# Loading x for TensorE's first transposes by 128-column blocks, with the first products between the transposes

## The chip, the cores and the metric

The kernel runs on one core of a Trainium2 chip. The metric is the device time of one execution in microseconds, lower is better. Each execution also leaves a span (first to last instruction, some 1.7 to 1.9 us less than the device time) and the mean TensorE clock that was granted. One execution of each kernel is profiled; all moments below are microseconds from the start of that profile's span.

## The reference, cut to what matters

```python
B, S, D, F = 32, 32, 1024, 3584          # bf16
def reference(x, w_gate, w_up, w_down):
    return (gelu(x @ w_gate) * (x @ w_up)) @ w_down
```

The tokens are 32 x 32 = 1024 rows. The kernel computes the products with one level of a Strassen-like scheme. The change touches the first 6 us alone.

## The kernel before

The products take x with its columns (d) on the partitions. Most of x is transposed while it is loaded. Such a load takes long (the first, issued at 2.2, has landed at 6.8), so the first 256 columns that are needed (KQ = 2 blocks of 128) are loaded as they lie, and TensorE transposes them: 4 row blocks x 2 column blocks = 8 transposes. VectorE and ScalarE copy the results from PSUM, the memory in which the transposes leave them, to `b21`. Six matmuls on constants (NWARM) run while these loads are on their way. The code is abridged; cuts are marked.

```python
NB = 512; P = 128; NB_P = 4; HALF = 2; KQ = 2; KB = 4; NWARM = 6
x_nat = spool.tile([P, NB_P, KQ * P], bf16, name="x_nat", tag="s1")
# SyncE's queue loads token rows 0..255, ScalarE's 256..511; both column blocks at once
for eng, p0, p1 in ((nc.sync, 0, HALF), (nc.scalar, HALF, NB_P)):
    eng.dma_start(out=x_nat[:, p0:p1, :], in_=xf[p0*P : p1*P, KD*P : (KD+KQ)*P].rearrange(...))
# ... (cut)
for k, eng in enumerate((nc.sync, nc.scalar)):
    load_ahead(0, k, k + 1, eng)            # weights a12a of k = 0 and k = 1
for which, eng in enumerate((nc.sync, nc.scalar)):
    load_w(eng, 0, which, KD, KD + KQ)      # first w_gate and w_up tiles
# ... (further loads cut)
for _ in range(NWARM):
    nc.tensor.matmul(warm_ps, lhsT=ones_w, rhs=ones_m, start=True, stop=True)
tags = iter("CCBB")
for dt in range(KQ):
    for half in range(2):
        tp = ps1.tile([P, HALF * P], bf16, name="tp", tag=next(tags), ...)
        for b in range(HALF):
            nc.tensor.transpose(tp[...], x_nat[:, half*HALF + b, dt*P : (dt+1)*P], ident)
        (nc.vector.tensor_copy, nc.scalar.copy)[half](b21[:, dt, ...], tp)
# ... (helpers cut)
ps = [acc(t) for t in "CCAA"]
for k in range(KQ):
    for cols in (first 256 tokens, last 256 tokens) if k == 0 else (all 512,):
        for j in range(KB):
            product_ahead(ps[j], 0, j, k, k + 1, cols)   # one matmul: a12a(k, j) x b21(k)
plain0(KD, KD + KQ)                          # first w_gate products, then w_up
```

The banks matter: `ps[0]` and `ps[1]` take the two C banks that the first two transposed halves used, so product j=1 cannot start before the second half has been copied.

## Time and profile before

| | before |
|---|---|
| time, median of 3 runs | 275.15 us (275.04 to 275.26) |
| span of the profiled run | 273.2 us |
| TensorE (PE) busy | 98% |
| first transpose / first product / first w_gate product | 3.49 / 4.34 / 6.35 us |
| full clock granted (clock record of the trace) | 4.89 us |

These are lines of the profile's page (the span, the busy table, and the summary of the chain of work that ended last).

```profile
span 273.2 us, 3351 instructions
...
PE 268.9 (98%) x1202; PEld 188.4 (69%) x1202; DVE 193.8 (71%) x194; ACT 112.1 (41%) x183; POOL 107.1 (39%) x55
...
PE 98%; ACT 0%; issue 0%
```

TensorE is the limit from end to end. The next fence is the timeline of TensorE in the head of the kernel before: start, duration, engine, line of the kernel, operation, output <- inputs, shape, type, count. Line L232 holds the transposes, L272 the first products, L239 the first w_gate and w_up products.

```profile
start us, us, engine line op out<-in xcount [idle before <-releaser]
2.86 0.63 PE L224 MATMUL psA<-const-bfloat16-1.0 128*128 128x512 bf16 x1
3.49 1.05 PE L232 MATMUL tp<-ident,x_nat 128*128 128x128 bf16 x8
4.34 0.63 PE L272 MATMUL psC<-b,a12a 128*128 128x256 bf16 x2
4.77 0.44 PE L272 MATMUL psA<-b,a12a 128*128 128x256 bf16 x2
5.05 0.38 PE L272 MATMUL psC<-b,a12a 128*128 128x256 bf16 x2
5.26 0.38 PE L272 MATMUL psA<-b,a12a 128*128 128x256 bf16 x2
5.48 0.59 PE L272 MATMUL psC<-b,a12a 128*128 128x512 bf16 x2
...
6.35 0.59 PE L239 MATMUL psA<-b,wg 128*128 128x512 bf16 x2
```

Read the starts, not the durations: matmuls overlap (a transpose is shown with 0.29 to 0.31 us, the next starts 0.107 us after it), and the end of one is modelled. Before the grant, transposes start 0.107 us apart and half-width products (256 tokens) 0.213 us apart. At full clock the distances are 0.055 and 0.109 us, half of that, so the state before the grant is called half clock here. Two products take 0.43 us at 4.34 and 0.22 us at 5.05: full clock was granted in between, at 4.89. The sixth warm-up starts at 2.86 and streams for 0.427 us (the distance between the starts of the warm-ups), to 3.29. So TensorE idled for 0.2 us before the first transpose, waiting for x:

```profile
PEld L232 <- DMA x_nat<-in_x_dram: 0.9, 1, 0.9
```

(From the table of waits: the weight load of the first transpose waited 0.9 us in total for the load of x, once; most of it passed while warm-ups still streamed.)

In the rest of this text, "idle" means TensorE's idle time between the last warm-up and the first w_gate product. It is computed from the starts and from the streaming times above, not from the modelled ends.

### The profile page before, as it was taken

The page shows a single profiled execution, that of the slowest core. Times are in us where ns is not written, and L with a number is a line of the kernel's source. Part 1 is how long each engine was busy: PE and PEld are TensorE (multiplying, and loading weights), DVE is VectorE, ACT ScalarE, POOL GpSimd, SP SyncE. Part 2 cuts the span into 40 slices and gives each one's busy share as a digit, 9 for nine tenths or more (in the row PEclk, how much of TensorE's full clock was granted, in tenths as well). Part 3 has the DMA queues.
Part 4 walks back from the last instruction along what each step waited for, and adds up shares of the span by engine and source line. Part 5 has one row for each costly group of instructions (what it writes and reads, how often), then busy time and mean ns, then how long its engine had stood idle before and what let it go on. Part 6 is the DMA issues. An engine that isn't in the chain of part 4 may idle for free.

```text
span 273.2 us, 3351 instructions
## 1 busy us (share of the span) xinstructions
PE 268.9 (98%) x1202; PEld 188.4 (69%) x1202; DVE 193.8 (71%) x194; ACT 112.1 (41%) x183; POOL 107.1 (39%) x55
## 2 busy tenths in 40 slices
PE   8999999999999999999999999999999999999994
PEld 4444777877877677676868686754447888888883
DVE  0268997986655676766658556459999999999511
ACT  2262665454643646555463636430300023962001
POOL 1000099999796794949577575000000000000000
PEclk9999999999999999999999999999999999999999
DMA  7994321423505505050514280005992445696202
GB/s 189 239 258 133 105 71 44 118 62 94 156 14 140 146 8 157 0 154 3 153 36 119 57 291 1 0 2 163 353 292 79 132 137 187 217 284 196 78 0 78
DMA packets 53249, 33.77 MB, mean 124 GB/s; under 512 B 8688, under 2 KB 53232, under 8 KB 53232
## 3 DMA queue, kind: packets, MB, share of 16 engines
q1 hardware_dynamic: 50240, 31.07, 39.7%
q10 hardware_dynamic: 2992, 2.49, 2.8%
q8 instruction: 9, 0.15, 0.2%
q14 instruction: 8, 0.07, 0.1%
HBM read 29.62 MB, written 2.10 MB: 116 GB/s over the span
## 4 chain that ended last, share of the span: by engine, by line
PE 98%; ACT 0%; issue 0%
PE psA L257 34%; PE psA L431 18%; PE psC L257 17%; PE psC L431 7%; PE psB L431 7%; PE psB L257 5%; PE psB L239 3%; PE psA L239 3%; PE psC L272 2%; PE psA L272 1%; PE psA L224 1%; PE tp L232 0%; ACT o_sb L571 0%
## 5 line engine op out<-in xcount | busy, mean ns | idle before, releaser
L257 PE MATMUL psA<-t,s 128*128 128x512 f32 x208 | 54.2, 402 | 0.0
L249 ACT ACTIVATE h<-c 128x512 bf16<-128x512 f32 x52 | 31.7, 627 | 37.4 <-DVE c L335 37.4
L257 PEld LDWEIGHTS psA<-t,s 128*128 128x128 f32 x208 | 39.1, 188 | 9.3
L162 POOL TENSOR_TENSOR s<-wu 128x1024 fp32r<-128x1024 bf16 x12 | 26.1, 2179 | 25.0 <-PE psC L257 16.8
L335 DVE TENSOR_TENSOR c<-sn,psA 128x512 f32<-128x512 f32 x26 | 17.7, 682 | 16.5 <-PE psA L257 14.6
L257 PEld LDWEIGHTS <-wg 128*128 128x128 bf16 x168 | 15.4, 98 | 20.2 <-issue 3.4
L163 POOL TENSOR_TENSOR s<-s,wg 128x1024 fp32r<-128x1024 f32 x12 | 27.4, 2284 | 0.9
L165 POOL TENSOR_TENSOR s<-wg,wu 128x1024 fp32r<-128x1024 bf16 x12 | 27.1, 2255 | 0.0
L340 ACT COPY sn<-psA 128x512 f32<-128x512 f32 x42 | 23.7, 584 | 7.9 <-PE psA L257 7.8
L257 PE MATMUL psA<-t,a22r 128*128 128x512 f32 x104 | 25.9, 391 | 0.0
L257 PE MATMUL psC<-t,s 128*128 128x512 f32 x104 | 25.8, 390 | 0.0
L257 PE MATMUL psC<-b22r,s 128*128 128x512 f32 x104 | 25.7, 389 | 0.0
L340 ACT COPY sn<-psC 128x512 f32<-128x512 f32 x26 | 15.2, 588 | 24.5 <-PE psC L257 22.7
L257 PE MATMUL psA<-b,wg 128*128 128x512 bf16 x104 | 24.6, 380 | 0.0
L257 PEld LDWEIGHTS psC<-t,s 128*128 128x128 f32 x104 | 19.4, 188 | 4.4 <-ACT ahead L362 0.3
L257 PEld LDWEIGHTS psA<-t,a22r 128*128 128x128 f32 x104 | 19.5, 188 | 4.1
L257 PEld LDWEIGHTS psC<-b22r,s 128*128 128x128 f32 x104 | 19.5, 188 | 4.1
L335 DVE TENSOR_TENSOR c<-sn,psC 128x512 f32<-128x512 f32 x26 | 17.7, 687 | 6.2 <-PE psC L257 6.2
L354 DVE TENSOR_TENSOR hi<-h,psA 128x512 bf16<-128x512 bf16 x14 | 9.6, 687 | 13.2 <-PE psA L257 13.2
L164 POOL TENSOR_TENSOR s<-wg,s 128x1024 fp32r<-128x1024 bf16 x8 | 17.2, 2155 | 0.6
L410 DVE TENSOR_TENSOR lo<-c,h 128x512 bf16<-128x512 f32 x12 | 16.9, 1405 | 0.6
L410 DVE TENSOR_TENSOR hi<-c,h 128x512 bf16<-128x512 f32 x14 | 16.9, 1205 | 0.5
(95 smaller groups left out, 398.5 us busy)
## 6 DMA issues: line engine op xcount, KB each, us to landing
wu<-in_w_up_dram SPq DMA_DIRECT2D x13, 512.0 KB, 4.1
wdb<-in_w_down_dram SPq DMA_DIRECT2D x12, 512.0 KB, 4.7
wdb<-in_w_down_dram SPq DMA_DIRECT2D x12, 384.0 KB, 4.2
wg<-in_w_gate_dram SPq DMA_DIRECT2D x8, 512.0 KB, 5.2
v<-in_w_down_dram SPq DMA_DIRECT2D x4, 512.0 KB, 6.1
out_dram<-o_sb ACTq DMA_DIRECT2D x16, 128.0 KB, 1.7
wg<-in_w_gate_dram SPq DMA_DIRECT2D x6, 256.0 KB, 4.5
v<-in_w_down_dram SPq DMA_DIRECT2D x4, 384.0 KB, 7.4
```

Of the source, the lines that this page charges most:

```text
L162: yield eng.tensor_tensor(s1, a21, a22, ADD)
L163: yield eng.tensor_tensor(s2, s1, a11, SUB)
L164: yield eng.tensor_tensor(s4, a12, s2, SUB)
L165: yield eng.tensor_tensor(s3, a11, a21, SUB)
L239: nc.tensor.matmul(ps, lhsT=w_tiles[0, which][:, dt, fl * P : (fl + 1) * P], rhs=x_rows(dt, nb), start=(dt == first), stop=(dt == last),)
L249: nc.scalar.activation(h, src, ACT.Gelu_apprx_tanh)
L257: nc.tensor.matmul(ps, lhsT=lhs[:, k, :], rhs=rhs[:, k, :], start=(start and k == 0), stop=(k == KD - 1), skip_group_check=True,)
L335: tt(t, s, ps, ADD)
L340: nc.scalar.copy(t, ps)
L354: tt(g_of(ft)[:, :NB], h0, psa, MUL)
L410: tt(g_of(ft)[:, NB:], added(sn5[fl], psa[fl]), h1[fl], MUL)
L431: nc.tensor.matmul(banks[m], lhsT=lhs(k)[:, m * P : (m + 1) * P], rhs=rhs(k), start=(start and k == 0), stop=(k == HF - 1), skip_group_che ...
```

## The change

The intent is to begin earlier. Only the first 128-column block of x is needed for the first products, so it is loaded alone, with half the bytes. TensorE transposes it, starts the k = 0 products on the first half of the tokens, transposes the second block, and goes on with the other half. All copies go to VectorE.

```diff
-        for eng, p0, p1 in ((nc.sync, 0, HALF), (nc.scalar, HALF, NB_P)):
+        def load_nat(eng, dt, p0, p1):
             eng.dma_start(
-                out=x_nat[:, p0:p1, :],
-                in_=xf[p0 * P : p1 * P, KD * P : (KD + KQ) * P].rearrange("(b p) d -> p b d", p=P),
+                out=x_nat[:, p0:p1, dt * P : (dt + 1) * P],
+                in_=xf[p0 * P : p1 * P, (KD + dt) * P : (KD + dt + 1) * P].rearrange("(b p) d -> p b d", p=P),
             )
+        load_nat(nc.sync, 0, 0, HALF)
+        load_nat(nc.scalar, 0, HALF, NB_P)
 ...
-        for k, eng in enumerate((nc.sync, nc.scalar)):
-            load_ahead(0, k, k + 1, eng)
+        load_ahead(0, 0, 1)
+        load_nat(nc.scalar, 1, 0, NB_P)
+        load_ahead(0, 1, 2, nc.scalar)
 ...
-        for dt in range(KQ):
+        def transposed(dt):
 ...
-                (nc.vector.tensor_copy, nc.scalar.copy)[half](b21[:, dt, half * hw : (half + 1) * hw], tp)
+                nc.vector.tensor_copy(b21[:, dt, half * hw : (half + 1) * hw], tp)
+        transposed(0)
 ...
         for k in range(KQ):
-            for cols in (slice(0, NB // 2), slice(NB // 2, NB)) if k == 0 else (slice(None),):
+            for half in range(2):
                 for j in range(KB):
-                    product_ahead(ps[j], 0, j, k, k + 1, cols)
+                    product_ahead(ps[j], 0, j, k, k + 1, slice(half * HALF * P, (half + 1) * HALF * P))
+                if k == half == 0:
+                    transposed(1)
```

More of the change, by code (lines that the diff above doesn't have):

```diff
@@ L183 @@
     with tc.manual_schedule():
-        for eng, p0, p1 in ((nc.sync, 0, HALF), (nc.scalar, HALF, NB_P)):
+        def load_nat(eng, dt, p0, p1):
             eng.dma_start(
-                out=x_nat[:, p0:p1, :],
-                in_=xf[p0 * P : p1 * P, KD * P : (KD + KQ) * P].rearrange("(b p) d -> p b d", p=P),
-            )
+                out=x_nat[:, p0:p1, dt * P : (dt + 1) * P],
+                in_=xf[p0 * P : p1 * P, (KD + dt) * P : (KD + dt + 1) * P].rearrange("(b p) d -> p b d", p=P),
+            )
+        assert KQ == 2
+        load_nat(nc.sync, 0, 0, HALF)
+        load_nat(nc.scalar, 0, HALF, NB_P)
         alloc_w(0, 0)
@@ L224 @@
             nc.tensor.matmul(warm_ps, lhsT=ones_w, rhs=ones_m, start=True, stop=True)
-        tags = iter("CCBB")
-        for dt in range(KQ):
+        def transposed(dt):
             for half in range(2):
                 hw = HALF * P
-                tag = next(tags)
+                tag = "CB"[dt]
                 tp = ps1.tile([P, hw], bf16, name="tp", tag=tag, bufs=BANKS[tag])
@@ L282, with plain0 @@
         ps = [acc(t) for t in "CCAA"]
-        tok0 = [(acc("A"), acc("B")) for _ in range(FC)]
-        def plain0(d0, d1):
+        def plain0(tok0, d0, d1):
             for which in (0, 1):
@@ L291 @@
         for k in range(KQ):
-            for cols in (slice(0, NB // 2), slice(NB // 2, NB)) if k == 0 else (slice(None),):
+            for half in range(2):
                 for j in range(KB):
-                    product_ahead(ps[j], 0, j, k, k + 1, cols)
-        plain0(KD, KD + KQ)
+                    product_ahead(ps[j], 0, j, k, k + 1, slice(half * HALF * P, (half + 1) * HALF * P))
+                if k == half == 0:
+                    transposed(1)
+        tok0 = [(acc("A"), acc("B")) for _ in range(FC)]
+        plain0(tok0, KD, KD + KQ)
         for j, copy in enumerate((nc.scalar.copy, nc.vector.tensor_copy) * 2):
@@ L300 @@
             copy(ahead[0][:, j, :], ps[j])
-        plain0(KD + KQ, DT)
+        plain0(tok0, KD + KQ, DT)
         a12_ahead.append(xpool.tile([P, KD, (NAHEAD - 2 * KB) * P], bf16, name="a12b"))
```

## The prediction

> **What bounds the kernel.** TensorE: 98% of the 273.2 us span (engine table), and the chain that ended last is 98% TensorE. From 3.49 us on, its first 25 us hold no wait. So only TensorE's idle or slow-clocked time in the head can change, and what changes there passes through one for one.
>
> **The head before (timeline, tiles, clock record).** Six warm-up matmuls start at 0.77, 0.427 us apart (half clock), and stop streaming at about 3.29. The halves of x land 2.7 and 2.9 us after issue (3.44, 3.63); the first transpose starts at 3.49. Eight transposes, 0.107 us apart, run to 4.34. The first copy (VectorE, 3.92 to 4.21, 0.29 us) hides under later transposes, so the first product starts at 4.34 with no gap. Full clock is granted at 4.89: half-width products go from 0.21 to 0.109 us. The first w_gate product starts at 6.35: my marker.
>
> **What the change does.**
> 1. First x loads: half the bytes, the same number of rows. Packets of 512 B take about 27 ns, of 256 B about 17 ns in this trace, but the first appear only 1.3 us after issue and come slower than the engines could take them, so I expect 0.05 to 0.15 us sooner, not half. [...] The unchanged warm-up ends at 3.29: at most 0.2 us to gain. Transposes start at about 3.40.
> 2. Four transposes stand before the first product, to 3.83. But nothing hides the copy now: second transpose + 0.31 us latency + 0.29 us copy + about 0.06 puts the first product at about 4.2, and its weights, landed at 4.24 before, come no sooner. A new TensorE gap of about 0.4 us. The second bank's copy, on VectorE after the first, ends at about 4.4, roughly as j=1 needs it.
> 3. The other four transposes move behind four half-width products, to about 5.0, at full clock (0.22 instead of 0.43 us). Block 1 of x lands at about 4.6, in time. Its copies hide under four products (0.44 us).
> 4. k=1 products are split: 4 more matmuls, a few ns each.
> 5. k=1 weights and first w_up tile go one place later in the ScalarE queue: about 5.1 (was 4.45) and 6.2 (was 5.78), needed at about 5.7 and 7.4. Later loads had about 0.5 us to spare.
>
> **Sum.** Before full clock TensorE streams for 1.4 us (3.49 to 4.89); after, about 1.08 (3.40 to 4.89 less 0.4). The lost 0.3 us of half-clock work costs 0.16 at full clock, plus small stalls: marker at 6.53 to 6.6. All on the critical path. Time 275.15 + 0.22 = 275.37 us, range 275.05 to 275.9.
>
> **Chances.** Faster by over 2%: 0.005; within 2%: 0.985; slower by over 2%: 0.01.
>
> **What would show it.** Timeline: first transpose 3.35 to 3.45 (1); TensorE idle 0.3 to 0.5 us after the fourth transpose, released by VectorE's copy or the weights (2); no wait at the later transposes (3), none for k=1 weights or w_up (5); marker 0.15 to 0.3 later; then both timelines parallel.
>
> **What would make it wrong.** The clock. [...] here it opened 4.1 us after the first matmul. [...] If it opens earlier or the gap is shorter, the change is level or gains 0.1. Block 1 landing after 5.0 would add its lateness one for one.

The sum came to 275.15 + 0.22 = 275.37 us. Passages are cut from the text, and the cuts marked, where no trace of this case shows what they said: a sentence on packet sizes in step 1, beside the packet times from the trace, and, under what would make it wrong, how the grant comes about and what a delay of it would cost, which was not part of the sum. The expectations of e1, e8 and e11 have cuts of the same kind.

## The result, and the profile after

| | before | after |
|---|---|---|
| time, median of 6 runs each, same rounds | 275.20 us (275.04 to 275.77) | 275.18 us (274.77 to 275.89) |
| ratio, 95% interval | | 0.9999 (0.9983 to 1.0014) |
| first transpose / first product / first w_gate product | 3.49 / 4.34 / 6.35 | 3.29 / 4.09 / 6.16 us |
| full clock granted | 4.89 us | 4.13 us |
| idle | 0.21 us | 0.45 us |

A ratio is the mean time of one kernel's runs over that of the other's of the same rounds, so it is not quite the ratio of the medians.

The page of the changed kernel:

```profile
span 273.0 us, 3360 instructions
...
PE 268.6 (98%) x1206; PEld 188.7 (69%) x1206; DVE 195.3 (72%) x196; ACT 110.9 (41%) x181; POOL 108.1 (40%) x55
...
PE 98%; ACT 0%; DVE 0%; issue 0%
```

TensorE's timeline in its head (here L237 are the transposes, L279 the first products, L246 the w_gate products):

```profile
3.29 0.63 PE L237 MATMUL tp<-ident,x_nat 128*128 128x128 bf16 x4
4.09 0.48 PE L279 MATMUL psC<-b,a12a 128*128 128x256 bf16 x2 [0.17 <-DVE b L240]
4.41 0.38 PE L279 MATMUL psA<-b,a12a 128*128 128x256 bf16 x2
4.62 0.39 PE L237 MATMUL tp<-ident,x_nat 128*128 128x128 bf16 x4
4.85 0.38 PE L279 MATMUL psC<-b,a12a 128*128 128x256 bf16 x2
...
6.16 0.81 PE L246 MATMUL psA<-b,wg 128*128 128x512 bf16 x3
```

The chain of work that ended last, in the same stretch (start, duration, what):

```profile
3.49 0.23 PE tp L237 x2
3.72 0.02 issue
3.74 0.30 DVE b L240
4.04 0.04 issue
4.09 0.48 PE psC L279 x2
```

The reader is to see three things. First, the transposes start as soon as the warm-up lets them, at 3.29. Second, VectorE's copy now stands in TensorE's chain, where before no copy did. The four transposes have streamed by 3.71, and the first product starts at 4.09: 0.37 us idle, and another 0.08 us before product j=1, whose bank waits for the second copy. Third, from the first products on the distances are those of full clock (4.41 to 4.62 for two).

So one number of the comparison is suspect. The changed kernel's w_gate products start 0.19 us earlier although TensorE idled 0.25 us longer, and the clock was granted 0.76 us earlier. The profiled run of the change, 274.77 us, is also the fastest of its six.

### An arithmetic for the head

From the first transpose to the first w_gate product TensorE streams 8 transposes and 16 half-widths: 8 x 0.107 + 16 x 0.213 = 4.27 us at half clock. At full clock each piece takes 0.51 of that (0.109/0.213). With O the moment of the grant, 3.29 the end of the warm-up, and I1 and I2 the idle time before and after O, the first w_gate product (the marker M) starts at

M = O + 0.51 x (4.27 - (O - 3.29 - I1)) + I2.

Before, with O = 4.885: 4.885 + 0.51 x (4.27 - 1.39) = 6.35 (measured 6.35). After, with O = 4.128: 4.128 + 0.51 x (4.27 - 0.47) + 0.08 = 6.15 (measured 6.16). Both fit. With before's O, the change would have reached the marker at 4.885 + 0.51 x (4.27 - 1.14) = 6.48, which is 0.13 later. With the change's O, before would have been at 5.98, which is 0.17 earlier than the change. These two are estimates from the measured numbers.

### The profile page after: what moved, and what is told of

Read it like the earlier page. It is cut to its first block, busy times and chain, and to the rows that moved or that the text cites. A ratio compares the mean times of both kernels' runs of the same rounds, so it can differ in the third digit from the quotient of the medians.

```text
span 273.0 us, 3360 instructions
## 1 busy us (share of the span) xinstructions
PE 268.6 (98%) x1206; PEld 188.7 (69%) x1206; DVE 195.3 (72%) x196; ACT 110.9 (41%) x181; POOL 108.1 (40%) x55
## 4 chain that ended last, share of the span: by engine, by line
PE 98%; ACT 0%; DVE 0%; issue 0%
PE psA L264 34%; PE psA L440 18%; PE psC L264 17%; PE psC L440 7%; PE psB L440 7%; PE psB L264 5%; PE psB L246 3%; PE psA L246 3%; PE psC L279 2%; PE psA L279 1%; PE psA L229 1%; ACT o_sb L580 0%; PE tp L237 0%; DVE b L240 0%
## 5 line engine op out<-in xcount | busy, mean ns | idle before, releaser
L162 POOL TENSOR_TENSOR s<-wu 128x1024 fp32r<-128x1024 bf16 x12 | 27.5, 2294 | 24.4 <-PE psC L264 16.0
L419 DVE TENSOR_TENSOR lo<-c,h 128x512 bf16<-128x512 f32 x12 | 17.9, 1490 | 0.6
L483 ACT COPY snb<-psC 128x512 f32<-128x512 f32 x4 | 2.2, 590 | 36.5 <-PE psC L440 36.5
```

The lines of the kernel that those rows point to most:

```text
L162: yield eng.tensor_tensor(s1, a21, a22, ADD)
L419: tt(g_of(ft)[:, NB:], added(sn5[fl], psa[fl]), h1[fl], MUL)
```

## The experiments

My theory has two parts. The change has the transposes start up to 0.2 us earlier and then idles longer than that, a small net loss. What the two profiles show the other way round is the moment of the clock grant, which is a matter of chance from run to run. The rivals are that the change itself makes the clock open earlier, that the change really gains 0.19 us, or that one of its two parts (loads, order) is a gain by itself. Runs e1 to e4 share their runs of before, and so do e5 to e8, and e9 to e11.

### e1: before again, unedited

> The kernel before, unedited, profiled a second time. My theory: the moment O at which full TensorE clock is granted is a matter of chance [...], and the first w_gate product (the marker M) follows it: M = 0.49 O + 3.97 us, from a first transpose at 3.49 and 4.27 us of half-clock work; O = 4.89 gave 6.35. So O will be another number than 4.89 and M will follow the formula within 0.1 us; the span follows as 273.19 + 0.49 (O - 4.89). Rival: the clock is granted earlier because of the change, then O is 4.89 here again.

Measured: full clock at 6.71 (it was 4.89), the first transpose at 3.28, M = 7.15, idle 0.02 us, span 274.0 us. From TensorE's timeline:

```profile
3.28 1.08 PE L232 MATMUL tp<-ident,x_nat 128*128 128x128 bf16 x8
...
6.71 0.60 PE L272 MATMUL psA<-b,a12a 128*128 128x512 bf16 x2
7.15 0.59 PE L239 MATMUL psA<-b,wg 128*128 128x512 bf16 x2
```

The time of the four runs was 275.13 to 275.85. The same program therefore moves its marker by 0.80 us by itself, and the span with it. My formula gave 7.26; it missed by 0.11 because x had landed at 3.23 instead of 3.44, so nothing was left to wait for. With the idle time as measured, the arithmetic above gives 7.15. What follows: O is not a property of the kernel, and before also can start its transposes the moment the warm-up ends. The head start of the change is 0 to 0.2 us.

### e2: the change again, unedited

> The changed kernel, unedited, profiled a second time. My theory: M = 0.49 O + 4.04 us (first transpose 3.29, a gap of 0.37 us after four transposes), plus up to 0.08 where the second product waits for the second copy; O will not be 4.13 again. At the same O this is 0.07 to 0.16 us later than before. Rival (the change lets the clock open sooner): O is 4.1 again and the marker 6.16. Second rival (the change gains 0.19 us, as the two profiles say): M at the same O lies 0.19 below before's.

Measured: O = 3.92, first transpose 3.28, first product 4.45, M = 6.48, idle 0.80 us, ratio 1.0007 (0.9986 to 1.0028). The size of the gap was wrong here. It was 0.74 us, and in the chain it is the weights, not the copy, that release the first product:

```profile
1.24 3.17 DMA a12a<-in_w_gate_dram
4.41 0.05 issue
4.45 0.39 PE psC L279 x2
```

The load was the same, and was issued at the same moment, as in the first profile of the change, where it landed at 3.73. By the arithmetic, this O and this idle time give 6.47. What follows: the grant came earlier than in the first profile, yet the marker is later. The change is exposed to a second thing: it has only four transposes, not eight, to fill the wait for the first weights. (Before had little to spare either. Its first weights landed at 4.25 and 4.09 in its two profiles, and its first product started at 4.34 and 4.15; by an estimate from these numbers, weights at 4.41 would have made it wait too, with 0.43 us, four transposes, less of idle time.) The rival "O is 4.1 again" is not refuted by this profile, since 3.92 is close to 4.13. It is taken up below the table of all heads.

### e3: the order of the change, the loads of before

```diff
-        load_nat(nc.sync, 0, 0, HALF); load_nat(nc.scalar, 0, HALF, NB_P)
+        for eng, p0, p1 in ((nc.sync, 0, HALF), (nc.scalar, HALF, NB_P)):
+            eng.dma_start(out=x_nat[:, p0:p1, :], ...)     # as before
```

The weights' loads follow in the order of before, too.

> The loads of before (both 128-column blocks of x in one load per half), TensorE's order and the copies of the change. My theory: first transpose at 3.49 as before, then the uncovered copy: a gap of about 0.37 us before the first product, M = 0.49 O + 4.15, 0.18 us later than before at the same O. Rival: the order is the useful part (fewer half-clock transposes), then M is at or below before's 0.49 O + 3.97.

Measured: O = 3.67, first transpose 3.29 (x had landed at 3.12), first product 4.09, idle 0.48 us (0.40 and 0.09, both released by VectorE's copies), M = 6.14; ratio 0.9994 (0.9977 to 1.0011).

```profile
3.29 0.58 PE L232 MATMUL tp<-ident,x_nat 128*128 128x128 bf16 x4
4.09 0.47 PE L274 MATMUL psC<-b,a12a 128*128 128x256 bf16 x2 [0.23 <-DVE b L235]
...
6.14 1.03 PE L241 MATMUL psA<-b,wg 128*128 128x512 bf16 x4
```

The gap came with the order alone, as expected. The first transpose was earlier than expected, because the loads of before landed earlier than in its first profile. My formula for M (5.95) assumed the idle time to lie before the grant, where it costs half; here all of it lay after, where it costs in full. The arithmetic gives 6.13.

### e4: the loads of the change, the order of before

> The loads of the change, TensorE's order and the copies of before. My theory: first transpose at 3.29 as in the change, but the fifth to eighth wait for block 1 (landed at 4.37 in the change): a gap of 0.6 to 0.7 us released by the load of x, M = 0.49 O + 4.2, 0.24 us later than before at the same O. Rival (the split loads alone are a gain of 0.2 us): M at 0.49 O + 3.87.

The edit: the split loads of the diff above, with the eight transposes in a row and the copies of before. Measured: the profiled run took 277.45 us, the four others 275.17 to 275.59; ratio 1.0003 (0.9984 to 1.0022). TensorE's timeline:

```profile
3.28 0.63 PE L237 MATMUL tp<-ident,x_nat 128*128 128x128 bf16 x4
4.91 0.61 PE L237 MATMUL tp<-ident,x_nat 128*128 128x128 bf16 x4 [0.99 <-DMA x_nat<-in_x_dram]
...
8.72 1.06 PE L244 MATMUL psA<-b,wg 128*128 128x512 bf16 x4
```

Block 1 landed at 4.86, so the gap was 1.20 us, not 0.65. The larger loss of the profiled run was elsewhere: full clock came at 8.78, after the whole head, which ran at half clock to its end. In the eight other profiles with six warm-ups the grant came between 3.67 and 6.71. What follows: no gain of the split loads alone was seen. The profile with the most idle time of these nine (1.17 us to the marker) also had the latest grant. That the one led to the other is my estimate; it was not shown (see e8).

### e5 and e6: both kernels with 20 warm-up matmuls

```diff
-    NWARM = 6
+    NWARM = 20
```

> Before with 20 warm-up matmuls instead of 6, so that every load has landed and full clock is granted before the first transpose: what is left is the order alone, at full clock. My theory: from the first transpose to the first w_gate product 2.46 us, of which 0.28 us TensorE idles (the first copy no longer hides under the transposes, which now take 0.45 us). Rival (the order of the change is as good, its gap came from late data): the same distance in the changed kernel. The whole time is longer by the warm-up and of no interest.

> The change with 20 warm-up matmuls. My theory: from the first transpose to the first w_gate product 2.70 us, 0.24 more than before with 20, all of it idle TensorE waiting for VectorE's first two copies (0.5 us in all). Rival: 2.46 us, as before with 20.

This takes away the landings and the grant: all has landed, and full clock is granted before the first transpose in both (3.48 and 6.70). What is left is the order. The lines of TensorE, before with 20:

```profile
6.45 0.61 PE L232 MATMUL tp<-ident,x_nat 128*128 128x128 bf16 x8
7.11 0.46 PE L272 MATMUL psC<-b,a12a 128*128 128x256 bf16 x2
...
8.92 1.03 PE L239 MATMUL psA<-b,wg 128*128 128x512 bf16 x4
```

and the change with 20:

```profile
8.02 0.38 PE L237 MATMUL tp<-ident,x_nat 128*128 128x128 bf16 x4
8.67 0.47 PE L279 MATMUL psC<-b,a12a 128*128 128x256 bf16 x2 [0.27 <-DVE b L240]
...
10.73 0.59 PE L246 MATMUL psA<-b,wg 128*128 128x512 bf16 x2
```

From the first transpose to the marker it is 8.918 - 6.449 = 2.47 us before and 10.728 - 8.019 = 2.71 us in the change (unrounded starts of the trace). Idle is 0.29 and 0.52 us. Expected were 2.46 and 2.70. With the landings and the grant taken out, the new order costs 0.24 us, all of it the uncovered copies. (The device times, 277.64 and 279.37, differ by the grant, which came 3.2 us later in e6 and left its warm-ups slow; single runs, state unknown.)

### e7: the change with 5 warm-up matmuls

> The change with 5 warm-up matmuls: block 0 of x landed at 2.9 in three profiles, the sixth warm-up streams to 3.29. My theory: the first transpose at 2.95 to 3.0, but the first product then waits for its weights (landed at 3.7 to 4.4) as well as for the copy, so it starts no sooner than 3.8: idle 0.5 to 0.9 us before the marker; of the 0.33 us taken out 0.1 at most shows in M, and the time stays within 0.5 us of before. Rival (the warm-up is all that hides the gain): M earlier by 0.17 us at the same O, no more idle time than the 0.45 of the change.

Measured: the profiled run took 277.28 us, the other three 274.97 to 275.27; ratio 1.0014 (0.9975 to 1.0053). The first transpose started at 2.86, 0.43 us earlier (2.95 to 3.0 was expected), and the first product at 4.29:

```profile
2.86 0.63 PE L237 MATMUL tp<-ident,x_nat 128*128 128x128 bf16 x4
4.29 0.61 PE L279 MATMUL psC<-b,a12a 128*128 128x256 bf16 x2 [0.80 <-DMA a12a<-in_w_gate_dram]
...
8.10 1.55 PE L246 MATMUL psA<-b,wg 128*128 128x512 bf16 x4
```

The weights landed at 4.24, so the earlier transposes only made the gap longer: idle 0.97 us, a little above the 0.5 to 0.9 expected, and 277.28 is outside the 0.5 us of before that I expected. Here too full clock came late, at 9.15. What follows: the warm-up does not hide a gain. Before 3.7 to 4.4 there is nothing for TensorE to multiply, since the first weights are not there.

### e8: the change with 2 warm-up matmuls

> The change with 2 warm-up matmuls: they stream to about 1.63, then TensorE idles to 2.95. [...] O lies between 6 and 10, mostly above 7, M between 7.5 and 8.7, and the time is 1 to 1.5 us above before's. Rival (the clock needs no activity beyond a fixed delay after the first matmul): O between 3.4 and 7 as before, and the time within 0.5 us of before's.

Measured: 275.67 to 278.02 us, median 277.08, ratio 1.0077 (1.0048 to 1.0106). The interval lies wholly above 1. O = 6.36 and M = 6.98 in the profiled run, which was the fastest of the four; expected were O between 6 and 10 (right) and M above 7.5 (wrong for this run). The median loss of 1.9 us is larger than the 1 to 1.5 us expected. The rival, a fixed delay after the first matmul with times within 0.5 us of before's, is out. This is the one experiment whose timing alone decides something: warm-up work, which computes nothing, is worth over a microsecond. Why it is so was not shown. The three slower runs were not profiled, and in the profiled run the grant, at 6.36, came within the range seen with six warm-ups, although TensorE idled from about 1.63 (an estimate: two warm-ups of 0.427 us from 0.77) to 2.99. The ground that this expectation gave for its O, M and time is cut; they stand as what was expected, no more.

Does idle time delay the grant? In the eight profiles with six warm-ups and a grant at 3.67 to 6.71, TensorE idled 0.02 to 0.80 us between the last warm-up and the marker. In e4 it idled 1.17 us, and the grant came at 8.78; in e7, with five warm-ups, it was 0.97 us and 9.15. That fits, but idle time alone does not put the grants in order: e1 idled 0.02 us and had 6.71, while the change in its first profile idled 0.37 us before a grant at 4.13. In e5 and e6 TensorE worked through the same warm-ups without a gap, and the grant came at 3.48 and 6.70. What decides the moment of the grant was not shown.

### e9: both blocks of x first, then the weights

```diff
         load_nat(nc.sync, 0, 0, HALF)
         load_nat(nc.scalar, 0, HALF, NB_P)
+        load_nat(nc.sync, 1, 0, HALF)
+        load_nat(nc.scalar, 1, HALF, NB_P)
 ...
-        load_nat(nc.scalar, 1, 0, NB_P)
 ...
         transposed(0)
+        transposed(1)
 ...
-                if k == half == 0:
-                    transposed(1)
```

> Both blocks of x before any weights (each block half on SyncE's and half on ScalarE's queue), eight transposes in a row as before, all copies on VectorE. My theory: block 1 lands by about 3.6, the copies hide again, and the gap that is left is the first weights', now third in their queue (landing 4.2 to 4.8): idle 0.1 to 0.5 us before the first w_gate product, no better than before's 0.02 to 0.21; time the same as before's within its spread of 1 us. Rival (the early block is worth its 0.2 us once the copies are hidden): first transpose 3.29, idle under 0.05, M = 0.49 O + 3.87.

Measured: eight transposes in a row from 3.29, first product at 4.70, idle 0.53 us (0.1 to 0.5 expected), O = 5.30, M = 6.73; ratio 1.0011 (0.9993 to 1.0029).

```profile
3.29 1.06 PE L238 MATMUL tp<-ident,x_nat 128*128 128x128 bf16 x8
4.70 0.61 PE L281 MATMUL psC<-b,a12a 128*128 128x256 bf16 x2 [0.35 <-DVE b L241]
```

Block 1 landed by 3.72 and the transposes ran without a gap, but the first weights, third in SyncE's queue, landed at 4.65. (The line names VectorE, whose fourth copy ended at 4.68. But the first product reads the first copy alone, which had ended at 4.04. And it started 0.046 us after the weights landed, as in e2 and e7, where the weights were the release; after a copy it is 0.052 to 0.053 us, as in the first profile of the change. So it was the weights.) This was my attempt at a version that beats both, and it does not: what is gained on x is given back on the weights.

### e10: the change, with the second half's copies on ScalarE

```diff
-                nc.vector.tensor_copy(b21[:, dt, ...], tp)
+                (nc.vector.tensor_copy, nc.scalar.copy)[half](b21[:, dt, ...], tp)
```

> The change, but the second half's copies on ScalarE as before. My theory: the second copy then ends at about 4.4 instead of 4.25 (ScalarE takes 0.37 us for one, VectorE 0.29), which holds the second product: idle before the marker 0.5 to 0.6 us instead of the change's 0.45 if the weights land by 4.1. Rival (VectorE doing both in turn is what makes the gap): idle below 0.4.

Measured: idle 0.57 us, in the range expected; the second product waited 0.23 us for ScalarE. The size was right, but not for the reason I gave. ScalarE's timeline:

```profile
2.82 1.28 ACT L240 ACT_TABLE_LOAD   x1 [2.82 <-issue]
4.11 0.37 ACT L240 COPY b<-tp 128x256 bf16<-128x256 bf16 x1
```

ScalarE first issues its loads, one more than before, then loads its function table for 1.28 us, and only then can copy, at 4.11. In before's profile the table load ran from 2.26 to 3.54, ahead of the first copy. So moving the copies to VectorE is the part of the change that keeps the fourth load on ScalarE's queue from showing. (One run of 276.05 us, state unknown.)

### e11: the change a third time

> The changed kernel, unedited, profiled a third time and timed in five more rounds. My theory: idle TensorE before the marker 0.45 us when the first weights land by 4.03 and more by their lateness after that (0.80 at 4.41); M follows from idle time and O by the same arithmetic as in all runs, and from M to the last matmul 262.97 to 263.03 us. Of some six runs none or one falls above 276.5 [...]. Rival (the idle time matters only through its own length): no run above 276.0 in any number of runs.

Measured: 274.93 to 275.97 us in six runs, ratio 1.0001 (0.9986 to 1.0016). O = 3.90, M = 6.27, idle 0.58 us, where 0.45 was expected with weights that landed by 4.03 (they had at 3.71): the 0.37 and 0.10 us of the two copies, and 0.09 us before k = 1, whose weights landed at 5.33 (5.10 in the first profile). No run passed 276.0, so a time like the 277.45 of e4 or the 277.28 of e7 was not seen in 16 runs of the change itself, and this experiment does not tell whether idle time matters only through its own length.

### All heads in one table

| profile | O | idle | M measured | M by the arithmetic |
|---|---|---|---|---|
| before | 4.89 | 0.21 | 6.35 | 6.35 |
| before again (e1) | 6.71 | 0.02 | 7.15 | 7.15 |
| after | 4.13 | 0.45 | 6.16 | 6.15 |
| after again (e2) | 3.92 | 0.80 | 6.48 | 6.47 |
| after, third (e11) | 3.90 | 0.58 | 6.27 | 6.25 |
| order only (e3) | 3.67 | 0.48 | 6.14 | 6.13 |
| loads only (e4) | 8.78 | 1.17 | 8.72 | 8.73 |

From M to the last matmul it is 262.97 to 263.04 us in all seven, and in e5, e6, e8 and e10. (The two exceptions are e9 with 263.16 and e7 with 263.50, where the clock came 1 us after M.) Nothing that happens in the head is caught up or made worse later, so idle time and O explain the span.

The three profiles of the change all had an early grant (4.13, 3.92 and 3.90), and the two of before a later one. Taken alone, this fits the rival that the change makes the clock open earlier. The timed runs speak against it. A run's mean granted clock was 0.997 or 0.998 in the profiles whose grant came at 6.36 to 6.71 (e1, e6, e8, e10; the time before a grant counts as 1.00 in this number, as 0 to 4.89 of before's profile does, so what is missing lies at the end: the grant then ended before the span did), and 1.000 in the six profiles with six warm-ups whose grant came at 3.67 to 5.30. Four of the 16 runs of the change show 0.998 (275.89 to 275.97 us, its slowest), and 11 of the 29 runs of before whose clock is listed show 0.997 or 0.998. So the change gets late grants too. Whether it gets them less often cannot be told from so few runs.

## Why the prediction was right or wrong, point by point

The time was predicted at 275.37 us (275.05 to 275.9) and within 2%; it is 275.18, ratio 0.9999 (0.9983 to 1.0014). The class and the range were right. The forecast loss of 0.22 us can neither be confirmed nor refuted by the timing: the runs of one unedited kernel spread over 1 us, and the interval is 0.4 us wide on either side. That the time fell into the range shows little, since five of the six runs of before in the table of the result lie in it as well. What the traces show is below.

1. **The landing of x: mis-sized.** I wrote 0.05 to 0.15 us sooner, to start at 3.40. SyncE's half landed at 2.92, 2.88 and 2.99 in the three profiles of the change, against 3.44 and 3.23 in the two of before, so 0.24 to 0.56 sooner (in e3, with before's loads, it landed at 3.12). The transposes started at 3.28 to 3.29, at the end of the warm-up. But before had one start at 3.28 too (e1), so the gain on TensorE is 0 to 0.2 us. (The landings in the prediction were worked out from durations with one decimal and are off by up to 0.05 us: ScalarE's half landed at 3.68, not 3.63. Packets of 256 B took 18 ns, not 17. Nothing hangs on either.)
2. **The new gap of about 0.4 us: right, and the main term.** It was 0.37 plus 0.08 us in the first profile, released by VectorE's copy, as written; 0.74 us in e2 where the weights landed late, which I had named as the second limit without giving its spread. I had them come no sooner than 4.24; they landed at 3.73, 4.41 and 3.71, so in two of the three profiles the copy was the limit. At full clock the order costs 0.24 us (e5, e6).
3. **Second block and its copies hidden: right** in the three profiles of the change, to within 0.02 us. The four transposes take 0.22 us at full clock.
4. **Four more matmuls for nearly nothing: right** (0.109 us per half-width throughout).
5. **Later places in ScalarE's queue harmless: right in the first profile** (k = 1 weights at 5.10, w_up at 5.96, no wait). In e11 the k = 1 weights came at 5.33 and cost 0.09 us.
6. **The marker at 6.53 to 6.6, "0.15 to 0.3 later": wrong in the profile**, which had 6.16, that is 0.19 earlier. The step that failed is the sum's "before full clock TensorE streams for 1.4 us (3.49 to 4.89); after, about 1.08 (3.40 to 4.89 less 0.4)": it took the 4.89 of one profile for a property of the kernel. The unedited before had 6.71 in its second profile, and the change had 4.13, 3.92 and 3.90. With O held at 4.89 the arithmetic puts the change at 6.48, an estimate that is 0.13 later, of the sign predicted and 0.05 us short of 6.53.
7. **What would make it wrong, a grant delayed by the new gap: not seen in the 16 runs of the change.** Its loads alone gave 277.45 once in five runs (e4), and five warm-ups 277.28 once in four (e7), with the grant at 8.78 and 9.15 in the trace. The idle time of the change was 0.45 to 0.80 us, against 1.17 and 0.97 us in those two. That the idle time delayed their grants was not shown, and whether an unlucky run of the change can have so late a grant is open.

So the large rearrangement moved the time little for a simple reason. The change took out at most 0.2 us of waiting for x and put in 0.4 to 0.8 us of waiting for a copy and for the weights. Idle time before the grant costs half its length, because what it displaces then runs at full clock, so by the arithmetic a loss of 0.13 us is left at the grant of before's profile (0.22 us where before's x lands as early as in e1). That is below what a spread of 1 us lets the timing show.

## What to carry to other kernels

Before splitting a load so that its first piece comes sooner, ask what else the first consumer waits for: here the copy from PSUM and the first weights stood right behind x, and a longer row of transposes had hidden the copy and covered most of the wait for the weights. When an effect is smaller than the spread of one unedited kernel, do not compare two profiles' moments; take the clock grant out first, by arithmetic or by a longer warm-up in both. Keep TensorE working through the head even on useless matmuls: with two warm-ups in place of six, the change took 277.08 us in the median against before's 275.14 in the same rounds (e8). A grant at 8.78 or 9.15 went with about 2 us more (277.45 against 275.17 to 275.59 in e4, 277.28 against 274.97 to 275.27 in e7). What brings the grant early was not shown.
